# Gated mix of two linear-attention blocks: another PSUM bank for the warm-ups and the gate's turn, and another order of the first k products

## The chip, the cores and the metric

One Trainium2 chip, and of it one core. The metric is the device time of one execution in microseconds (us). The kernel before took 183.33 us, the median of 3 executions (183.22 to 184.1). A profile is one further execution, recorded instruction by instruction; its times are counted from the first instruction of the span.

## The reference

The input `x` has 2048 rows of 640 columns in bf16. Two blocks, A and B, with weights of their own, both read this `x`. Each block makes q, k and v with one product, applies the feature map `phi` to q and k, and does linear attention over 32 heads of 20 columns. A gate, one number for each row, mixes the two results.

```python
g = _sigmoid((x * gate_w).sum(-1, keepdims=True))
a = _A_ref(x, A_wqkv, A_wo)
b = _B_ref(x, B_wqkv, B_wo)
return g * a + (1 - g) * b

# a block (H = 32 heads of Dh = 20):
qkv = (x @ wqkv).reshape(B, S, 3, H, Dh).transpose(2, 0, 3, 1, 4)
q, k, v = qkv[0], qkv[1], qkv[2]
phi = lambda t: jnp.where(t > 0, t + 1, jnp.exp(t)) + 1e-6
pq, pk = phi(q), phi(k)
kv = jnp.einsum("bhsd,bhse->bhde", pk, v)
z = jnp.einsum("bhsd->bhd", pk)
num = jnp.einsum("bhqd,bhde->bhqe", pq, kv)
den = jnp.einsum("bhqd,bhd->bhq", pq, z)[..., None] + 1e-6
return (num / den).transpose(0, 2, 1, 3).reshape(B, S, D) @ wo
```

The gate's logit of a row is the product of that row of `x` with `gate_w`. The kernel gets it as one more column of A's k product.

## The kernel before

`x` is cut into 16 row chunks of 128 (index `i`) and its 640 columns into 5 column chunks of 128 (index `c`). TensorE contracts over the partitions, so every product needs `x` transposed: the tile `xT`, 128 x 5 x 2048. DMA transposes write most of `xT`. The first two row chunks are loaded as they are (`xn`) and turned on TensorE: five 128x128 transposes for each chunk, into the PSUM tiles `turned[0]` and `turned[1]` (named `xt` in the profile), which VectorE copies to `xT` in two pieces each, column chunks 0 and 1 first and 2 to 4 after (`keep`, line 242).

PSUM has eight banks. The pool `psum` gives them out as four slots of two banks (line 55); a tile in a slot may be written only when the tile that had the slot before has been read for the last time. Which instruction has to wait for that is worked out when the program is built. Before the change, slot 3 holds the tile `warm`: seven products of ones with ones (line 160) that keep TensorE at work while the first loads are under way, and later, in the second bank of the same tile, the turned gate column (line 256). Slot 3 is then given to the second chunk's k accumulator (line 260). Slot 2 holds the first chunk's, and slots 0 and 1 hold `turned`.

A k product (`k_mm`, line 214) takes one column chunk of one row chunk as weights and streams 320 columns of `wk[0]`, the weights of A's k; `hf` says which half of its 640 columns, and each half has a PSUM bank of its own. The second half is 321 wide, because column 640 of `wk[0]` holds `gate_w`. A row chunk so takes ten products: five column chunks by two halves.

How that gate column gets there matters below. `gate_w` is loaded as five rows of 128 into a corner of the tile `R` (line 131). `gate_column` (line 162) then turns these 5 rows on TensorE into 128 x 5 in PSUM, copies this to `gsb` with VectorE, and copies it with GpSimd, one column chunk at a time (five copies, line 168), into column 640 of `wk[0]`. Every product of the second half reads that column, so it must not start before GpSimd has written it for its column chunk.

The loads are issued on two queues. SyncE's has: `x` chunk 0, `wk` column chunks 0, 2 and 4, DMA transposes of the chunks 2 and 3, `wq` in three parts, and the other transposes of `x`. ScalarE's has: `x` chunk 1, `wk` column chunk 1, `gate_w`, `wk` column chunk 3.

The stage that the change touches is `k_first` (line 232), written in the order in which it is to run (`tc.manual_schedule`). On TensorE its order before is, with c for column chunk, h for half and i for row chunk: ten transposes; c0 h0 i0; the gate's turn; c1 h0 i0; c0 h0 i1; c1 h0 i1; then c0 and c1 of the second half for both row chunks; c2 in both halves; c3 and c4 of row chunk 0; c3 and c4 of row chunk 1. After these come the row chunks 2 and 3 (`k_chunk`, line 225), and then the q products, first in `q_block` (line 284). On VectorE the order before is: `keep` of c0 and c1 for both row chunks, the copy to `gsb`, `keep` of c2 to c4 for both.

Of the kernel before, what the change touches and what calls it, by code (L numbers as in the profile page):

```python
# [9 lines left out]
FP32 = mybir.dt.float32  # L10
# [6 lines left out]
DT = D // P  # L17
# [3 lines left out]
HB = 512  # L21
# [10 lines left out]
def kernel(  # L32
# [11 lines left out]
    nc = tc.nc  # L44
# [13 lines left out]
    def ps_raw(name, slot=None):  # L58

        if slot is None:  # L60
            slot = turn[0]
            turn[0] = (slot + 1) % 4
        return psum.tile([P, 4 * HB], BF16, tag=f"ps{slot}", name=name)

    def ps(name, slot=None):

        return ps_raw(name, slot).bitcast(FP32).rearrange("p (b n) -> p b n", b=2)
# [85 lines left out]
        )  # L153


    raw = ps_raw("warm", 3)
    warm = raw.bitcast(FP32).rearrange("p (b n) -> p b n", b=2)
    one_l, one_r = [nc.const_aps.tensor(1.0, [P, n], BF16) for n in (P, HB)]
    for n in (HB,) * 6 + (HB // 2,):
        nc.tensor.matmul(warm[:, 0, 0:n], lhsT=one_l, rhs=one_r[:, 0:n], start=True, stop=True)  # L160

    def gate_column(gcol):

        nc.tensor.transpose(out=gcol, in_=grow, identity=ident[0:DT, 0:DT])
        gsb = work.tile([P, DT], BF16, tag="rT", name="gsb")
        nc.vector.tensor_copy(out=gsb[:], in_=gcol)
        for c in range(DT):
            nc.gpsimd.tensor_copy(out=wk[0][:, c, D:D + 1], in_=gsb[:, c:c + 1])
# [45 lines left out]
    def k_mm(b, i, c, pt, hf):  # L214
        w = HF + (hf if b == 0 else 0)
        nc.tensor.matmul(  # L216
            pt[:, hf, 0:w], lhsT=xT[:, c, i * P:(i + 1) * P], rhs=wk[b][:, c, hf * HF:hf * HF + w],
            start=(c == 0), stop=(c == DT - 1),
        )

    def k_done(b, i, pt, lifted=False):
        side = (lambda: nc.scalar.copy(out=logit[:, i:i + 1], in_=pt[:, 1, HF:HF + 1])) if b == 0 else None
        phi(pk[:, i, :].rearrange("p (b n) -> p b n", b=2), pt[:, :, 0:HF], HF, lifted, side)

    def k_chunk(b, i, slot=None, lifted=False):
        pt = ps(f"k{'AB'[b]}", slot)
        for hf in range(2):
            for c in range(DT):
                k_mm(b, i, c, pt, hf)
        k_done(b, i, pt, lifted)  # L230

    def k_first():

        pts = [ps("kA", 2), None]
        turned = [ps_raw("xt", i) for i in range(2)]

        def turn(i):
            for c in range(DT):
                cols = slice(c * P, (c + 1) * P)
                nc.tensor.transpose(out=turned[i][:, cols], in_=xn[:, i, cols], identity=ident[:])  # L240

        def keep(i, lo, hi):
            src = turned[i][:, 0:D].rearrange("p (c n) -> p c n", c=DT)
            nc.vector.tensor_copy(out=xT[:, lo:hi, i * P:(i + 1) * P], in_=src[:, lo:hi])

        def part(cs, hfs, chunks=(0, 1)):
            for c in cs:
                for hf in hfs:
                    for i in chunks:
                        k_mm(0, i, c, pts[i], hf)  # L250

        for i in range(2):
            turn(i)
            keep(i, 0, 2)
        part((0,), (0,), (0,))
        gate_column(raw[:, 2 * HB:2 * HB + DT])
        for i in range(2):
            keep(i, 2, DT)
        part((1,), (0,), (0,))
        pts[1] = ps("kA", 3)  # L260
        part((0, 1), (0,), (1,))
        part((0, 1), (1,))
        part((2,), (0, 1))
        for i in range(2):
            part((3, 4), (0, 1), (i,))
            k_done(0, i, pts[i])
        for i in range(2, CB):
            k_chunk(0, i, i - 2)
# [272 lines left out]
    part = [slice(n * RB, (n + 1) * RB) for n in range(4)]  # L541
# [156 lines left out]
    with tc.manual_schedule():  # L698
        k_first()
# [23 lines left out]
    with tc.manual_schedule():  # L723
# [101 lines left out]
        for i in range(half - 1):  # L825
            p, after = pairs[i:i + 2]
# [48 lines left out]
```

## Time and profile before

| what | us |
|---|---|
| median of 3 executions (183.22, 183.33, 184.1) | 183.33 |
| the profiled execution, from its first to its last instruction (span) | 181.9 |
| what lies around the span, by the median | 1.4 |
| busy time in the span: TensorE products | 177.9 |
| busy time in the span: TensorE weight loads, beside the products | 120.7 |
| busy time in the span: VectorE | 147.2 |
| busy time in the span: ScalarE | 86.3 |
| busy time in the span: GpSimd | 2.5 |

The profiled execution's time is known by its span alone; its share before the first and after the last instruction is taken from the median. PE is TensorE's products, PEld its weight loads, DVE is VectorE, ACT ScalarE, POOL GpSimd, SP SyncE; a q behind an engine's name is its queue or sequencer, which issues DMAs. In a timeline row the first number is when the first instruction of the row started, the second how long the row lasts until its last instruction ends; `xN` is the count. The duration of a product counts from its start to the arrival of its last result, and products overlap, so that the distance between two starts, not the duration, is what one product costs in a stream.

### The profile page before, as it was taken

The page shows a single profiled execution, that of the slowest core. Times are in us where ns is not written, and L with a number is a line of the kernel's source. Part 1 is how long each engine was busy: PE and PEld are TensorE (multiplying, and loading weights), DVE is VectorE, ACT ScalarE, POOL GpSimd, SP SyncE. Part 2 cuts the span into 40 slices and gives each one's busy share as a digit, 9 for nine tenths or more (in the row PEclk, how much of TensorE's full clock was granted, in tenths as well). Part 3 has the DMA queues.
Part 4 walks back from the last instruction along what each step waited for, and adds up shares of the span by engine and source line. Part 5 has one row for each costly group of instructions (what it writes and reads, how often), then busy time and mean ns, then how long its engine had stood idle before and what let it go on. Part 6 is the DMA issues. An engine that isn't in the chain of part 4 may idle for free.

```text
span 181.9 us, 3296 instructions
## 1 busy us (share of the span) xinstructions
PE 177.9 (98%) x1285; PEld 120.7 (66%) x1285; DVE 147.2 (81%) x248; ACT 86.3 (47%) x141; POOL 2.5 (1%) x18
## 2 busy tenths in 40 slices
PE   8999999999999999999999999999999999999993
PEld 3566657765577777877775555577778777777772
DVE  0386868989998896788778999969799999877863
ACT  2245846889961101378784779921102863111010
POOL 4100000000000000000000000000000000000000
PEclk9999999999999999999999999999999999999999
DMA  5899999423100116241115000000343570133323
GB/s 177 207 248 189 224 373 310 85 52 130 58 0 8 67 45 211 77 137 37 56 34 191 17 0 0 0 0 18 126 105 84 174 188 0 40 108 108 114 90 126
DMA packets 22598, 19.17 MB, mean 105 GB/s; under 512 B 10294, under 2 KB 21814, under 8 KB 22582
## 3 DMA queue, kind: packets, MB, share of 16 engines
q1 hardware_dynamic: 20644, 16.82, 33.4%
q10 hardware_dynamic: 1938, 2.13, 3.5%
q8 instruction: 10, 0.16, 0.4%
q14 instruction: 6, 0.05, 0.1%
HBM read 12.13 MB, written 4.53 MB: 92 GB/s over the span
## 4 chain that ended last, share of the span: by engine, by line
PE 95%; DMA 2%; ACTq 0%; DVE 0%; issue 0%
PE gs L369 17%; PE kA L216 12%; PE ox L583 12%; PE kB L216 12%; PE qB L280 12%; PE qA L280 6%; PE oz L583 6%; PE qA L290 5%; PE gB L328 2%; PE gA L328 2%; PE ow L583 2%; DMA R<-in_gate_w_dram 2%; PE qA L300 1%; PE s L485 1%; PE mA L485 1%; PE kvA L455 1%
## 5 line engine op out<-in xcount | busy, mean ns | idle before, releaser
L216 PEld LDWEIGHTS <-xT 128*128 128x128 bf16 x320 | 31.1, 98 | 12.5 <-issue 0.2
L208 DVE TENSOR_SCALAR e<-e 128x640 bf16<-128x640 bf16 (+2 forms) x53 | 18.9, 357 | 8.1 <-ACT e L203 7.4
L216 PE MATMUL kB<-wkB,xT 128*128 128x320 bf16 x160 | 23.0, 299 | 0.0
L216 PE MATMUL kA<-wkA,xT 128*128 128x320 bf16 (+1 forms) x160 | 22.6, 300 | 0.2 <-DMA wkA<-in_A_wqkv_dram 0.2
L280 PE MATMUL qB<-xT,wqB 128*128 128x512 bf16 x100 | 21.7, 379 | 0.0
L203 ACT ACTIVATE e<-kB 128x640 bf16<-128x640 f32 x16 | 11.3, 704 | 16.2 <-DMA wqB<-in_B_wqkv_dram 9.4
L280 PEld LDWEIGHTS <-wqB 128*128 128x128 bf16 x100 | 11.7, 117 | 9.7
L203 ACT ACTIVATE e<-kA 128x640 bf16<-128x640 f32 x16 | 11.2, 705 | 8.5 <-PE kA L216 8.5
L203 ACT ACTIVATE e<-qA 128x1024 bf16<-128x1024 f32 (+1 forms) x11 | 10.4, 946 | 6.4 <-PE qA L290 5.1
L633 ACT COPY u<-ox 128x320 f32<-128x320 f32 x8 | 3.4, 426 | 20.4 <-PE ox L583 20.4
L203 ACT ACTIVATE e<-qB 128x1024 bf16<-128x1024 f32 x10 | 10.2, 1024 | 5.6 <-PE qB L280 4.9
L369 PEld LDWEIGHTS <-xn 128*128 128x128 bf16 x96 | 9.2, 98 | 3.9 <-issue 0.4
L369 PEld LDWEIGHTS <-S 128*128 128x128 bf16 x96 | 9.4, 98 | 3.6
L280 PE MATMUL qA<-xT,wqA 128*128 128x512 bf16 x50 | 11.0, 379 | 0.0
L212 DVE SCALAR_TENSOR_TENSOR pk<-kB,e 128x640 bf16<-128x640 f32 x12 | 9.9, 825 | 1.3
L583 PEld LDWEIGHTS <-xT 128*128 128x128 bf16 x85 | 8.1, 98 | 2.9
L583 PEld LDWEIGHTS <-pqTB 128*128 128x128 bf16 x80 | 7.8, 98 | 3.2
L583 PEld LDWEIGHTS <-pqTA 128*128 128x128 bf16 x80 | 7.7, 98 | 2.9
L369 PE MATMUL gs<-pk,xn 128*128 128x320 bf16 x64 | 9.5, 299 | 0.0
L280 PEld LDWEIGHTS <-wqA 128*128 128x128 bf16 x50 | 5.9, 117 | 4.8
L290 PE MATMUL qA<-xT,wqA 128*128 128x512 bf16 x40 | 9.0, 379 | 0.0
L210 DVE TENSOR_TENSOR pk<-pk,e 128x640 bf16<-128x640 bf16 x12 | 5.9, 493 | 2.8 <-ACT pk L207 2.1
(122 smaller groups left out, 297.7 us busy)
## 6 DMA issues: line engine op xcount, KB each, us to landing
out_dram<-pk SPq DMA_DIRECT2D x14, 160.0 KB, 1.8
xn<-in_A_x_dram SPq DMA_DIRECT2D x3, 640.0 KB, 6.3
wkB<-in_B_wqkv_dram SPq DMA_DIRECT2D x1, 800.0 KB, 4.6
wqB<-in_B_wqkv_dram ACTq DMA_DIRECT2D x1, 800.0 KB, 5.1
wvB<-in_B_wqkv_dram SPq DMA_DIRECT2D x1, 800.0 KB
MA<-mA_dram SPq DMA_DIRECT2D x1, 800.0 KB, 4.2
MB<-mB_dram SPq DMA_DIRECT2D x2, 400.0 KB, 4.5
wqA<-in_A_wqkv_dram SPq DMA_DIRECT2D x2, 320.0 KB, 4.2
```

What stands on the lines that cost most here:

```text
L203: nc.scalar.activation(out=e[:], in_=src, func=ACT.Exp)
L208: nc.vector.tensor_scalar(e[:], e[:], 1.0, EPS, op0=ALU.min, op1=ALU.add)
L210: nc.vector.tensor_tensor(out=dst, in0=dst, in1=e[:], op=ALU.max)
L212: nc.vector.scalar_tensor_tensor(out=dst, in0=src, scalar=1.0 + EPS, in1=e[:], op0=ALU.add, op1=ALU.max)
L216: nc.tensor.matmul(pt[:, hf, 0:w], lhsT=xT[:, c, i * P:(i + 1) * P], rhs=wk[b][:, c, hf * HF:hf * HF + w], start=(c == 0), stop=(c == DT - 1),
L280: nc.tensor.matmul(pt[:, u, :], lhsT=mixed(wq[b][:, c, :], m), rhs=xT[:, c, n * HB:(n + 1) * HB], start=(c == 0), stop=(c == DT - 1),)
L290: nc.tensor.matmul(pt[:, u, :], lhsT=mixed(wq[b][:, c, :], m + u), rhs=xT[:, c, n * HB:(n + 1) * HB], start=(c == 0), stop=(c == DT - 1),)
L328: nc.tensor.matmul(pt[:, hf, 0:HF], lhsT=xn[:, i, c * P:(c + 1) * P], rhs=pk[:, i, hf * HF:(hf + 1) * HF], start=(i == 0), stop=(i == ST - 1),
L369: nc.tensor.matmul(pt[:, n, 0:HF], lhsT=left[:, i, n * P:(n + 1) * P], rhs=right[:, i, :], start=(first and i == 0), stop=(i == hc - 1), s ...
L485: nc.tensor.matmul(dst[:w, 0:HF], lhsT=KVA[:w, k, 0:w], rhs=wo_sb[b][:w, k, n * HF:(n + 1) * HF], start=True, stop=True,)
L583: nc.tensor.matmul(dst, lhsT=left[:, c, r0:r0 + P], rhs=right[:, c, :], start=(first and c == 0), stop=(c == DT - 1), skip_group_check=not ...
L633: nc.scalar.copy(out=self.u6[:], in_=self.at("x"))
```

## The change

The seven warm-up products and the gate's turn now write the second bank of slot 1, the slot of `turned[1]`, whose transposes take only the first bank. Slot 3 has no other tile ahead of the second chunk's k accumulator any more, so both accumulators can be written from the start. The order in `k_first` is new as well. On TensorE: ten transposes; c0 and c1 of the first half for both row chunks (four products); the gate's turn; c2 h0 i0; c0 and c1 of the second half for both row chunks; c2 h0 i1; c2 h1 for both; and then c3 and c4 as before. On VectorE `keep` of c2 to c4 of row chunk 0 now stands ahead of the copy to `gsb`, and that of row chunk 1 behind it. The number of instructions on every engine is the same, and from c3 of row chunk 0 on TensorE's order is as before; ScalarE, GpSimd and SyncE have the same instructions in the same order throughout.

```diff
-    raw = ps_raw("warm", 3)
-    warm = raw.bitcast(FP32).rearrange("p (b n) -> p b n", b=2)
+    opened = [ps("kA", slot) for slot in (3, 2)]
+    pts = opened[::-1]
+    turned = [ps_raw("xt", i) for i in range(2)]
+    warm = turned[1].bitcast(FP32).rearrange("p (b n) -> p b n", b=2)
     one_l, one_r = [nc.const_aps.tensor(1.0, [P, n], BF16) for n in (P, HB)]
     for n in (HB,) * 6 + (HB // 2,):
-        nc.tensor.matmul(warm[:, 0, 0:n], lhsT=one_l, rhs=one_r[:, 0:n], start=True, stop=True)
+        nc.tensor.matmul(warm[:, 1, 0:n], lhsT=one_l, rhs=one_r[:, 0:n], start=True, stop=True)
...
     def k_first():
 
-        pts = [ps("kA", 2), None]
-        turned = [ps_raw("xt", i) for i in range(2)]
-
...
         for i in range(2):
             turn(i)
             keep(i, 0, 2)
-        part((0,), (0,), (0,))
-        gate_column(raw[:, 2 * HB:2 * HB + DT])
-        for i in range(2):
-            keep(i, 2, DT)
-        part((1,), (0,), (0,))
-        pts[1] = ps("kA", 3)
-        part((0, 1), (0,), (1,))
+        part((0, 1), (0,))
+        keep(0, 2, DT)
+        gate_column(turned[1][:, 2 * HB:2 * HB + DT])
+        keep(1, 2, DT)
+        part((2,), (0,), (0,))
         part((0, 1), (1,))
-        part((2,), (0, 1))
+        part((2,), (0,), (1,))
+        part((2,), (1,))
         for i in range(2):
             part((3, 4), (0, 1), (i,))
             k_done(0, i, pts[i])
```

## The prediction

> **What bounds the kernel now.** I read the page first, then the chain of waits, and then the timeline of the one stage that the change touches. On the page TensorE decides:
>
> ```profile
> span 181.9 us, 3296 instructions
> PE 177.9 (98%) x1285; PEld 120.7 (66%) x1285; DVE 147.2 (81%) x248; ACT 86.3 (47%) x141; POOL 2.5 (1%) x18
> ...
> PE 95%; DMA 2%; ACTq 0%; DVE 0%; issue 0%
> ```
>
> TensorE's products are busy for 98% of the span, and the chain that ended last is TensorE for 95% and DMA for 2%. So a time won or lost on TensorE early on goes through to the end, unless a later wait eats it. Nearly all of the DMA's 2% is one load (3.71 of 181.9 us). The start of the chain of waits (start, length, what):
>
> ```profile
> 1.73 3.71 DMA R<-in_gate_w_dram
> 5.44 0.05 issue
> 5.49 0.17 PE warm L164
> 5.66 0.24 PE kA L216
> 5.91 0.01 issue
> 5.92 5.34 PE kA L216 x38
> 11.26 4.32 PE qA L290 x20
> ```
>
> The load of `gate_w`, issued at 1.73, lands at 1.73 + 3.71 = 5.44; the gate's turn starts at 5.49; and from 5.92 TensorE runs without a stop. All that the change can move lies between 5.05 and about 7.3 us. The timeline of that stretch (start, length, engine, line, work, count, idle time before):
>
> ```profile
> 3.62 1.25 PE L240 MATMUL xt<-ident,xn 128*128 128x128 bf16 x10
> ...
> 4.38 0.29 DVE L244 COPY xT<-xt 128x256 bf16<-128x256 bf16 x1 [3.40 <-PE xt L240]
> 4.72 0.10 PEld L216 LDWEIGHTS <-xT 128*128 128x128 bf16 x1
> 4.91 0.29 DVE L244 COPY xT<-xt 128x256 bf16<-128x256 bf16 x1 [0.24 <-PE xt L240]
> 5.05 0.30 PE L216 MATMUL kA<-wkA,xT 128*128 128x320 bf16 x1 [0.17 <-DMA wkA<-in_A_wqkv_dram]
> 5.49 0.09 PEld L164 LDWEIGHTS <-R 5*128 5x128 bf16 x1 [0.66 <-DMA R<-in_gate_w_dram]
> 5.49 0.17 PE L164 MATMUL warm<-ident,R 5*128 5x5 bf16 x1
> ...
> 5.60 1.98 PE L216 MATMUL kA<-wkA,xT 128*128 128x320 bf16 x12
> 5.70 0.16 DVE L166 COPY gsb<-warm 128x5 bf16<-128x5 bf16 x1 [0.50 <-PE warm L164]
> 5.78 0.61 DVE L244 COPY xT<-xt 128x384 bf16<-128x384 bf16 x2
> ...
> 5.93 0.66 POOL L168 COPY wkA<-gsb 128x1 bf16<-128x1 bf16 x5 [3.45 <-DVE gsb L166]
> ```
>
> And single instructions of it, from the same view over a few hundredths of a us each (a product of the first half, GpSimd's first copy, and where the second half and where c3 begin):
>
> ```profile
> 5.60 0.31 PE L216 MATMUL kA<-wkA,xT 128*128 128x320 bf16 x1
> 5.93 0.19 POOL L168 COPY wkA<-gsb 128x1 bf16<-128x1 bf16 x1 [3.45 <-DVE gsb L166]
> 6.19 0.43 PE L216 MATMUL kA<-wkA,xT 128*128 128x321 bf16 x2
> 7.28 0.44 PE L216 MATMUL kA<-wkA,xT 128*128 128x320 bf16 x2
> ```
>
> Read in order: product 1 at 5.05, the gate at 5.49, product 2 at 5.60, product 3 at 5.92, product 5, the first of the second half, at 6.19, product 13, the first of c3, at 7.28. From product 5 to 13 are eight steps in 7.28 - 6.19 = 1.09 us: **0.136 us is what a k product costs** in a stream (its 0.30 us of duration overlap). Twelve products at that price are 1.63 us; the stretch from 5.05 to 7.28 takes 2.23. So TensorE stands still for about 0.6 us, less the gate's own slot (5.60 - 5.49 = 0.11): **0.49 us is what the stretch could give** at most.
>
> Where that stands: from 5.05 + 0.14 = 5.19 to 5.49, 0.30 us, TensorE has only the gate next, whose weights come by DMA; from 5.60 + 0.14 = 5.74 to 5.92, 0.18 us, product 3 waits until slot 3 is free, that is for the copy to `gsb`, which ends at 5.70 + 0.16 = 5.86.
>
> **The change part by part.** *The spare bank.* The seven warm-ups and the gate's turn are the same instructions at another address, and before the transposes nothing else touches slot 1: 0. Product 3's wait for slot 3 goes.
>
> *Four products ahead of the gate.* Product 1 stays at 5.05, because it waits for `wk` column chunk 0. The second is now c0 of row chunk 1, and its weights come with VectorE's second copy, which ends at 4.91 + 0.29 = 5.20. From the first such copy's end, 4.38 + 0.29 = 4.67, to the weight load at 4.72 it took 0.05, so product 2 starts at 5.25. The third needs `wk` column chunk 1. Its issue, and the answer for that issue in the view of DMAs (last number: us to landing):
>
> ```profile
> 1.24 0.46 ACTq L123 DMA_DIRECT2D wkA<-in_A_wqkv_dram x1
> wkA<-in_A_wqkv_dram ACTq DMA_DIRECT2D x1, 160.0 KB, 4.0
> ```
>
> It lands at 1.24 + 4.0 = 5.24, before it is wanted: products 3 and 4 start at 5.39 and 5.53, and the gate's turn at **5.66** in place of 5.49. `gate_w` has long landed then (5.44).
>
> *VectorE.* The copy that now stands ahead of `gsb` is one of 384 columns. Two of them took 0.61 us, so one at most 0.35. It can start when the 256-column copy ends at 5.20 and is done by 5.55, before the gate is turned; so it does not hold up `gsb`. The other moves behind `gsb`, ends near 6.3, and is wanted for the eleventh product only, at about 6.9.
>
> *The product that fills in.* After the gate comes c2 h0 i0, at 5.66 + 0.11 = 5.77. Its weights are there at 5.55 + 0.05 = 5.60. Its `wk` column chunk 2:
>
> ```profile
> 1.73 0.42 SPq L123 DMA_DIRECT2D wkA<-in_A_wqkv_dram x1
> wkA<-in_A_wqkv_dram SPq DMA_DIRECT2D x1, 160.0 KB, 3.9
> ```
>
> 1.73 + 3.9 = 5.63, in time. TensorE is free again at 5.77 + 0.14 = 5.91.
>
> *What is late next: the gate column.* The sixth product is the first of the second half, and it reads the column that GpSimd writes. Before, from the gate's start to the end of GpSimd's first copy it took 5.93 + 0.19 - 5.49 = 0.63 us, by way of `gsb` at 5.70. With a semaphore's 0.05 the column could be read at 6.17, and the product that reads it began at 6.19: a wait without cost, with 0.02 to spare. Now the same 0.68 us count from 5.66, and the column can be read at **6.34**, while TensorE is free at 5.91. So a new wait of **0.43 us** stands where the two old gaps (0.30 and 0.18) were. Behind it in TensorE's queue are all the others; none can pass. GpSimd's further copies follow at (0.66 - 0.19) / 4 = 0.12 us, faster than TensorE asks for them, and cost nothing.
>
> *The sum.* Seven products stand between that wait and c3: c0 and c1 of the second half (four), c2 h0 i1, c2 h1 for both. 6.34 + 7 x 0.136 = 7.29. Before it was 7.28. **The stage ends within 0.02 us of where it ended**: the gate begins 0.17 later, and against this one product fewer (0.136) is left to do behind the gate column. From c3 on the order is as before. Against the profiled execution that is 181.9 + 0.02 = 181.9 in the span, and with the 1.4 us around it, 183.33 - 181.9, **183.35** against the median of the three runs.
>
> *Bounds.* From below: were TensorE never to wait after 5.25, c3 would begin at 5.77 + 8 x 0.136 = 6.86, 0.42 earlier. That can't be reached while the second half reads a column that comes 0.68 us behind the gate. From above: the gate's turn now stands behind `wk` column chunk 1, which in the shown run came 0.15 before it was wanted. Were it to land as late as the next one, 5.63, products 3 and 4 would start at 5.68 and 5.82, the gate at 5.95, and c3 at 5.95 + 0.68 + 0.95 = 7.58, 0.30 later. So the stage itself lies between -0.42 and +0.30.
>
> **What could hide a gain, or make a loss larger.** The q products follow at 11.09 to 11.26. The first part of their weights:
>
> ```profile
> 6.50 0.58 SPq L136 DMA_DIRECT2D wqA<-in_A_wqkv_dram x1
> wqA<-in_A_wqkv_dram SPq DMA_DIRECT2D x1, 320.0 KB, 4.2
> ```
>
> They land at 6.50 + 4.2 = 10.7, so up to about 0.4 us of gain would meet no wait there; a forecast of 0 never comes near it. SyncE's queue waits only for landings and not for TensorE, so no transfer moves.
>
> **The clock.** TensorE's rate changes within this stretch, though the page grants 1.00 throughout. The seven warm-ups, the q products at full stream, the last warm-up alone, and one stage of the view of windows (stage and its length, busy PE, PEld, DVE, ACT, POOL, then the granted clock):
>
> ```profile
> 0.84 2.93 PE L160 MATMUL warm<-const-bfloat16-1.0 128*128 128x512 bf16 x7 [0.84 <-PEq L859]
> 11.09 4.48 PE L290 MATMUL qA<-xT,wqA 128*128 128x512 bf16 x20
> ...
> 3.35 0.42 PE L160 MATMUL warm<-const-bfloat16-1.0 128*128 128x256 bf16 x1
> ...
> 3.00:4.00 1.00, 1.00 (x7) 0.46 (x6) 0.00 (x0) 1.00 (x1) 0.00 (x0) 1.00 1.04 342
> ```
>
> A warm-up costs about (2.93 - 0.42) / 6 = 0.42 us for 512 columns, a q product 4.32 / 20 = 0.216. So TensorE started at half its rate, and the k products at 0.30 us each ran at the full one already at 5.05. Up to there both kernels issue the same work at the same times. The Trainium skill, "TensorE: Matmul & The Clock Gate", Part 1, tells of a clock that is doubled only after a busy window of some 3.4 us that runs freely, whatever the kernel does, and halved after an idle one; the trace agrees as to the step of two and its time. By that rule a pause of half a microsecond changes nothing, but a window that is judged too idle would put off the full rate by another one, 1.7 us at half price, or 185.0 as an estimate.
>
> **The rivals.**
>
> *A. Even trade* (forecast): as summed, 183.35, c3 within 0.1 us of 7.28. For it: the times of the five links from the gate to the column stand in the trace, and they are latencies of idle engines, not shares of busy ones.
>
> *B. A net gain of 0.1 to 0.4 us, 183.0 to 183.2.* If `gate_w` lands later in most executions than in this one, say after 5.62, the gate starts at the same time in both kernels, and the change keeps one product fewer behind it: 0.14 us. More would need a shorter way from the gate to the column, for which no row speaks.
>
> *C. It doesn't do what it says: fewer than four products are ahead in time*, because column chunk 1 of `wk` or the second copy is late and the gate waits behind them: +0.1 to +0.3, 183.45 to 183.65. For it: the margin is 0.15 us on a transfer that takes 4.0. Against it: it is issued 0.49 us before `gate_w`.
>
> *D. Slower beyond doubt: the full rate comes later.* The change puts one pause of 0.43 us in place of 0.30 and 0.18. If what decides on the clock looked at that very stretch, the products after 5.91 would run at half rate, and each us of that costs 0.5. A loss of 0.92 us needs 1.84 us of it. As long a stretch again as from the first warm-up to the first product at full rate, 5.05 - 0.84 = 4.2 us, would cost 2.1: 185.4. Against it: the full rate was there at 5.05, and afterwards pauses of 0.30 and 0.18 us didn't end it.
>
> *E. Faster beyond doubt*: the same the other way round. One of the three runs before took 184.1, 0.8 more than the others; if that were a later full rate and the change made it rarer, the median would still be 183.2 to 183.3. So 0.9 us is not to be had here, other than by a cause that I don't see.
>
> **How the numbers follow.** Chances: A 0.62, B 0.12, C 0.16, D 0.06, E 0.04. About 0.5% of the time, 0.92 us, is what a measurement of this kernel can tell from no change: the three runs before differ by 0.88. A, B and C all lie within it, 0.90 together; D is slower, E faster. The range: A to C give 183.0 to 183.65; the runs before spread from 183.22 to 184.1 without any change, so I take 182.8 to 184.0.
>
> **What would show it.** In the profile of the changed kernel: the gate's turn near 5.66 and no longer in a pause; a pause of some 0.4 us on TensorE ahead of the first 321-wide product, put down to GpSimd's copy or to issue; that product near 6.34; c3 of row chunk 0 near 7.29; q products from 11.1 on as before. Wrong would be: c3 before 7.1 or after 7.5, k products 0.27 us apart in place of 0.136 after 5.05, or a new wait after 7.3.

## The result, and the profile after

| | before | changed |
|---|---|---|
| median, us (22 executions each) | 183.38 (183.05 to 184.1) | 183.91 (183.32 to 184.38) |
| ratio to before, 95% interval | | 1.0025 (1.0015 to 1.0034) |
| profiled execution: span, us | 181.9 | 182.4 |
| profiled execution: time, us | not listed | 184.13 |

The forecast was 183.35, no change, with a range of 182.8 to 184.0. The time lies in the range and within 0.5%, but the change is slower by 0.28 to 0.62 us, which repeated executions do tell from zero. The range held the time only because it had been widened by the scatter of the runs before: the rivals A to C alone ended at 183.65.

The page of the changed kernel (it has five product records fewer than the page of before, at the same number of weight loads):

```profile
span 182.4 us, 3291 instructions
...
PE 178.1 (98%) x1280; PEld 120.7 (66%) x1285; DVE 147.2 (81%) x248; ACT 86.2 (47%) x141; POOL 2.5 (1%) x18
...
PE 94%; issue 3%; POOL 1%; DVE 0%; POOLq 0%
```

TensorE still decides. In place of the DMA's 2%, the chain's start is now put down to issue and to GpSimd, as the end of that start in the chain of waits shows (start, length, what):

```profile
2.47 4.16 issue
6.63 0.21 POOLq L868
6.84 0.04 issue
6.88 4.93 PE kA L218 x35
```

TensorE's unbroken stream begins at 6.88, not at 5.92, and what it waited for is GpSimd's copy of the gate column. (The link from there to `gsb` is lost in this view; the timeline has it.) The timeline of the stage in the changed kernel:

```profile
4.75 1.51 PE L218 MATMUL kA<-wkA,xT 128*128 128x320 bf16 x4
4.94 0.56 DVE L243 COPY xT<-xt 128x256 bf16<-128x256 bf16 x2 [0.24 <-PE xt L239]
5.28 0.40 PEld L218 LDWEIGHTS <-xT 128*128 128x128 bf16 x3 [0.43 <-DVE xT L243]
6.19 0.10 PEld L166 LDWEIGHTS <-R 5*128 5x128 bf16 x1 [0.52 <-issue]
6.20 0.18 PE L166 MATMUL xt<-ident,R 5*128 5x5 bf16 x1
...
6.31 0.31 PE L218 MATMUL kA<-wkA,xT 128*128 128x320 bf16 x1
6.42 0.17 DVE L168 COPY gsb<-xt 128x5 bf16<-128x5 bf16 x1 [0.93 <-PE xt L166]
...
6.65 0.66 POOL L170 COPY wkA<-gsb 128x1 bf16<-128x1 bf16 x5 [4.18 <-DVE gsb L168]
6.88 1.39 PE L218 MATMUL kA<-wkA,xT 128*128 128x321 bf16 x9 [0.26 <-POOL wkA L170]
```

The order is the forecast's: four products, the gate, one product, a wait for GpSimd, the second half. The times are not. The four products take 1.51 us from start to end where four at full rate without a wait take about 0.7 (3 x 0.136 + 0.30): the second waits for VectorE's second copy until 5.28, and the others run at half rate. The gate's turn starts at 6.20, where 5.66 was forecast. It waits for no load: its weights stand behind "issue". In this execution `gate_w` had landed at 4.68, by the trace's semaphore events, which the views list only where something waits for them. Before, it had landed at 5.44.

All of the difference lies in this stage. The first product of row chunk 2, one instruction each from the timelines of the kernel before and of the changed one:

```profile
8.37 0.57 PE L216 MATMUL kA<-wkA,xT 128*128 128x320 bf16 x3
```

```profile
8.93 0.57 PE L218 MATMUL kA<-wkA,xT 128*128 128x320 bf16 x3
```

8.93 - 8.37 = 0.56, and the spans differ by 0.55. Behind that product, span less start, it is 173.49 us in both; in all the 14 profiles of this study it lies between 173.48 and 173.57. Each profile can therefore be read by its first nine microseconds alone:

| profile | `gate_w` landed | full rate from | gate's turn | first 321-wide | c3 | row chunk 2 |
|---|---|---|---|---|---|---|
| before | 5.44 | 4.82 | 5.49 | 6.19 | 7.28 | 8.37 |
| e5, before again | 4.83 | 4.43 | 5.14 | 5.84 | 6.93 | 8.02 |
| changed | 4.68 | 6.35 | 6.20 | 6.88 | 7.84 | 8.93 |
| e4, changed again | 4.67 | 4.16 | 5.51 | 6.19 | 7.14 | 8.23 |
| e1, gate first | 4.80 | 5.81 | 5.42 | 6.33 | 7.29 | 8.38 |
| e2, gate after one | 4.76 | 6.24 | 5.37 | 6.38 | 7.33 | 8.43 |
| e3, gate after two | 4.80 | 5.75 | 5.70 | 6.55 | 7.50 | 8.60 |
| e6, after one, slot 0 | 4.54 | 3.83 | 4.77 | 5.86 | 6.81 | 7.93 |
| e7, no column read | 4.71 | 4.05 | 5.43 | 5.79 | 6.73 | 8.04 |
| e8, 128-row gate | 4.67 | 6.57 | 6.16 | 6.88 | 7.83 | 8.93 |
| e9, before, late `gate_w` | 6.45 | 4.16, again 10.99 | 6.50 | 7.20 | 8.96 | 11.05 |
| e10, changed, late `gate_w` | 6.95 | 5.57 | 7.00 | 7.67 | 8.63 | 9.72 |
| e11, before, one warm-up | 4.64 | about 7.1 | 5.16 | 6.08 | 7.70 | 8.79 |
| e12, changed, one warm-up | 4.80 | about 7.5 | 6.26 | 6.95 | 8.14 | 9.23 |

The full rate's start is the trace's clock event. For e11 and e12 it is read from the distance of the products. In e7's row the product under "first 321-wide" is 320 wide.

### The profile page after: what moved, and what is told of

Its sections match the earlier page's. It is cut to its first block, busy times and chain, and to the rows that moved or that the text cites. A ratio compares the mean times of both kernels' runs of the same rounds, so it can differ in the third digit from the quotient of the medians.

```text
span 182.4 us, 3291 instructions
## 1 busy us (share of the span) xinstructions
PE 178.1 (98%) x1280; PEld 120.7 (66%) x1285; DVE 147.2 (81%) x248; ACT 86.2 (47%) x141; POOL 2.5 (1%) x18
## 4 chain that ended last, share of the span: by engine, by line
PE 94%; issue 3%; POOL 1%; DVE 0%; POOLq 0%
PE gs L367 17%; PE ox L581 12%; PE kB L218 12%; PE qB L278 12%; PE kA L218 12%; PE qA L278 6%; PE oz L581 6%; PE qA L288 5%; PE gB L326 2%; PE gA L326 2%; PE ow L581 2%; PE qA L298 1%; PE s L483 1%; PE mA L483 1%; PE kvA L453 1%
## 5 line engine op out<-in xcount | busy, mean ns | idle before, releaser
L218 PE MATMUL kA<-wkA,xT 128*128 128x320 bf16 (+1 forms) x160 | 23.3, 304 | 0.3 <-POOL wkA L170 0.3
```

The costliest lines, as they stand in the source:

```text
L218: nc.tensor.matmul(pt[:, hf, 0:w], lhsT=xT[:, c, i * P:(i + 1) * P], rhs=wk[b][:, c, hf * HF:hf * HF + w], start=(c == 0), stop=(c == DT - 1),
```

## The experiments

Two theories stood against each other at first. "Place": what stands ahead of the gate's turn on TensorE delays the gate column, and the second half waits for that. "Clock": the new bank or the new pause puts off TensorE's full rate.

**e1, e2, e3: the gate's turn behind none, one and two products, spare bank and own slots kept; e4: the changed kernel again.** The three edits in one, abridged:

```diff
+        gate_column(...)            # e1: here
         part((0,), (0,), (0,))
+        gate_column(...)            # e2: here
         part((0,), (0,), (1,))
+        gate_column(...)            # e3: here
         part((1,), (0,))
         keep(0, 2, DT)
-        gate_column(turned[1][:, 2 * HB:2 * HB + DT])
```

In e1 to e3 both `keep` of c2 to c4 follow the gate.

> Spare bank and own slots as in the change, but the gate's turn ahead of all k products. Theory 'place' (the gate column is what the second half waits for, and what stands ahead of the gate's turn on TensorE decides): the gate starts as soon as gate_w has landed (4.7 to 5.4 us), first 321-wide product near 6.3, c3 near 7.25, time -0.15 to 0.0 us against the kernel before, about 0.5 us under the changed kernel. Theory 'clock' (warm-ups and gate's turn in the other bank put off TensorE's full rate): +0.3 to +0.6 us against before, as the changed kernel, with k products still 0.27 us apart after 5.3.

> Spare bank and own slots as in the change, the gate's turn behind one k product as before the change, then the other three, c2 h0 i0 and the second half. 'Place': gate at 5.1 to 5.5, no wait for GpSimd's column, c3 near 7.1 to 7.3, -0.16 to -0.05 us against before. 'Clock': +0.3 to +0.6 us.

> The same with two k products ahead of the gate's turn. 'Place': between e2 and the changed kernel, -0.15 to +0.1 us against before; where TensorE is at half rate by then the gate starts near 5.7. 'Clock': +0.3 to +0.6 us.

> The changed kernel once more, on the same chip as the three others, to have its times beside theirs and a second profile of it. Both theories: +0.3 to +0.6 us against before. 'Place': whether the profile shows the four products 0.27 or 0.136 us apart depends on when the full rate comes in that execution; the gate starts near 6.2 where they are 0.27 apart, near 5.7 to 5.8 where they are not. 'Clock': the full rate comes after 6 us again.

| | median, us | ratio to before, 95% interval |
|---|---|---|
| e1, gate first | 183.53 | 1.0027 (1.0001 to 1.0052) |
| e2, after one | 183.39 | 1.0004 (0.9992 to 1.0015) |
| e3, after two | 183.77 | 1.0017 (1.0008 to 1.0027) |
| e4, after four, the change | 183.62 | 1.0017 (1.0006 to 1.0029) |

(Before, on the same chip: 183.34.) With one product ahead the time is that of before; with two and four it is slower. With none the interval only just leaves 1 out. The spare bank and the own slots, which e2 has as well, don't by themselves make the change's loss: "clock" as the banks' doing falls. The full rate came at 5.81, 6.24, 5.75 and 4.16 us in the four profiles, the earliest in the changed kernel itself, so the change does not force the 6.35 of its first profile.

Three of the four sizes were missed all the same: e2 didn't gain its 0.05 to 0.16 us, e1 gained nothing, and e3 lost as much as the change. Not all of e3's loss is its two products:

```profile
6.15 0.66 POOL L170 COPY wkA<-gsb 128x1 bf16<-128x1 bf16 x5 [3.68 <-DVE gsb L168]
6.40 1.07 PEld L218 LDWEIGHTS <-xT 128*128 128x128 bf16 x9 [0.47 <-DVE xT L243]
```

The fill-in product c2 h0 i0 had to wait for VectorE's copy, which in e3 stands behind the one to `gsb`, and started at 6.40. The column could be read near 6.39 (6.15 + 0.19, and 0.05 from the copy's end to its reader), so by an estimate from these rows about 0.16 us of e3's loss, the first 321-wide product at 6.55 and not at 6.39, belongs to VectorE's order.

e1's timeline shows why the gate is not early there:

```profile
4.96 0.10 PEld L166 LDWEIGHTS <-R 5*128 5x128 bf16 x1 [0.20 <-DMA R<-in_gate_w_dram]
5.07 0.29 DVE L243 COPY xT<-xt 128x256 bf16<-128x256 bf16 x1 [0.24 <-PE xt L239]
5.42 0.16 PE L166 MATMUL xt<-ident,R 5*128 5x5 bf16 x1 [0.38 <-DVE xT L243]
```

The weights are in at 4.96, but the turn waits 0.38 us for VectorE's second copy, which still reads the other bank of the same tile. That is a cost of the spare bank that the prediction had put at 0. The change's own order doesn't pay it, because its second product waits for the same copy anyway. Why two of e1's twelve executions took 185.45 and 185.48 stays open; one of the eleven of e5, the kernel before unaltered, took 185.57.

e4's time is as expected; its gate, expected at 5.7 to 5.8 where the full rate comes early, started at 5.51. Its timeline has the changed kernel at full rate from its first product on:

```profile
4.72 0.86 PE L218 MATMUL kA<-wkA,xT 128*128 128x320 bf16 x4
...
5.51 0.09 PEld L166 LDWEIGHTS <-R 5*128 5x128 bf16 x1 [0.26 <-issue]
5.51 0.17 PE L166 MATMUL xt<-ident,R 5*128 5x5 bf16 x1
...
5.72 0.16 DVE L168 COPY gsb<-xt 128x5 bf16<-128x5 bf16 x1 [0.52 <-PE xt L166]
...
5.94 1.64 PE L218 MATMUL kA<-wkA,xT 128*128 128x320 bf16 x10 [0.25 <-DVE gsb L168]
...
5.95 0.66 POOL L170 COPY wkA<-gsb 128x1 bf16<-128x1 bf16 x5 [3.48 <-DVE gsb L168]
```

Here the four products take 0.86, and the gate starts at 5.51 though `gate_w` had been there since 4.67. (The 0.25 ahead of the fifth product ended with `wk` column chunk 2, landed at 5.90; the view names `gsb`, done at 5.88.)

**e5: the kernel before, unaltered, to see whether its first profile was typical.**

> The kernel before once more, as it stands: what two sets of times of one kernel differ by, and a second profile. Theory 'landing' (in the profile that the prediction was made from, gate_w landed at 5.44 us, later than in most executions; in the five profiles since it landed at 4.67 to 4.80): gate_w near 4.7, the gate's turn at 5.0 to 5.2 instead of 5.49, the first 321-wide product near 5.9 to 6.2 and c3 of row chunk 0 at 7.0 to 7.4, the later the later the full rate comes. Rival 'order alone' (landing as in the first profile, the changed kernel loses elsewhere): gate at 5.49 again. Time: within 0.15 us of the kernel before.

Median 183.44 (before, in this set: 183.34), ratio 1.0014 (0.9993 to 1.0036): two sets of one kernel. Its timeline:

```profile
4.90 0.31 PE L216 MATMUL kA<-wkA,xT 128*128 128x320 bf16 x1
5.14 0.09 PEld L164 LDWEIGHTS <-R 5*128 5x128 bf16 x1
5.14 0.17 PE L164 MATMUL warm<-ident,R 5*128 5x5 bf16 x1
...
5.25 2.39 PE L216 MATMUL kA<-wkA,xT 128*128 128x320 bf16 x15
5.35 0.16 DVE L166 COPY gsb<-warm 128x5 bf16<-128x5 bf16 x1 [0.21 <-PE warm L164]
...
5.58 0.66 POOL L168 COPY wkA<-gsb 128x1 bf16<-128x1 bf16 x5 [3.10 <-DVE gsb L166]
```

The gate starts at 5.14 and waits for no load; the first 321-wide product and c3 come 0.06 and 0.07 us before the times named. `gate_w` landed at 4.83 here. Twelve profiles issue that load where the kernel before does; in eleven of them it landed at 4.54 to 4.83, and the twelfth is the one that the prediction was read from. This execution took 183.34 us, the median of before; its span is 181.6.

**e6: as e2, the gate's turn in the second bank of slot 0.**

```diff
-        gate_column(turned[1][:, 2 * HB:2 * HB + DT])
+        gate_column(turned[0][:, 2 * HB:2 * HB + DT])
```

> As e2, gate's turn behind one k product, but written into the second bank of slot 0 (the first chunk's transposes) in place of slot 1. In e1 and e2 the gate's turn waited for VectorE's second copy out of slot 1, to 5.37 and 5.42 us, though gate_w had landed at 4.8. 'Landing': the gate starts at 5.0 to 5.2, 0.2 earlier than in e2, and the stage has no wait left behind it: c3 at 7.0 to 7.25, -0.2 to 0.0 us against before, the fastest so far. Rival 'gate doesn't matter': as e2, +0.07 us.

Median 183.25, ratio 0.9998 (0.9983 to 1.0012). The gate starts at 4.77, with no wait for VectorE, and c3 at 6.81, the earliest of all kernels that read the column:

```profile
4.77 0.17 PE L166 MATMUL xt<-ident,R 5*128 5x5 bf16 x1
```

Both came earlier than named. So the wait in e1 and e2 was the shared tile's. The time is the lowest median of the experiments, but no difference to before can be told. Its interval lies below the changed kernel's (1.0015 to 1.0034) and overlaps e4's (1.0006 to 1.0029), so that it beats the changed kernel is likely, and that it beats before is not shown.

**e7: the second half of the first two row chunks 320 wide.** It leaves out the gate's logits of 256 rows, with the two ScalarE copies that fetch them.

```diff
-        w = HF + (hf if b == 0 else 0)
+        w = HF + (hf if b == 0 and i > 1 else 0)
...
-        side = (lambda: ...) if b == 0 else None
+        side = (lambda: ...) if b == 0 and i > 1 else None
```

> The changed kernel, but the second half of the first two row chunks is 320 wide and so doesn't read the gate column (the gate's logits of these 256 rows are left out, with the two copies that fetch them). 'Landing' and 'place': the wait of 0.3 to 0.6 us ahead of the second half goes, c3 0.25 to 0.6 us earlier than in the changed kernel, time -0.3 to +0.1 us against before. Rival 'half rate' (the loss is that more products run at half rate): no such gain, +0.3 us or more.

Median 183.44, ratio 0.9995 (0.9973 to 1.0017). With the gate as late as in e4 (5.43), c3 comes 0.41 us earlier (6.73 against 7.14): the column's wait is where the stage loses. Not all of the 0.41 is the column's, since loads and first products scatter (`wk` column chunk 2 landed at 5.61 here and at 5.90 in e4). Within e7 the column could have been read 0.68 behind the gate, at 6.11, and the product started at 5.79: 0.32 us. The time alone doesn't show it: the interval touches the changed kernel's. Half of the gain is given back at once:

```profile
8.04 0.39 PEld L218 LDWEIGHTS <-xT 128*128 128x128 bf16 x4 [0.39 <-DMA xT<-in_A_x_dram]
```

Row chunk 2 waits for its DMA transpose, landed at 7.99 here and at 7.44 to 8.0 in all profiles. That is the next wall. By an estimate from these landings (0.05 from landing to start, and 8 x 0.136 from c3 to row chunk 2), a c3 earlier than 6.4 (landing at 7.44) to 6.95 (landing at 8.0) brings nothing.

**e8: the gate's turn with 128 rows of weights.**

```diff
+    nc.vector.memset(R[0][:, 0:P], 0.0)
-        nc.tensor.transpose(out=gcol, in_=grow, identity=ident[0:DT, 0:DT])
+        nc.tensor.matmul(gcol, lhsT=R[0][:, 0:P], rhs=ident[:, 0:DT], start=True, stop=True)
...
-        gate_column(turned[1][:, 2 * HB:2 * HB + DT])
+        gate_column(warm[:, 1, 0:DT])
```

> The changed kernel, but the gate's turn is a plain product with all 128 rows (the corner of R is zeroed first, five columns of the identity are streamed). In both profiles of the changed kernel the gate's turn, whose weights have 5 rows, started 0.09 to 0.14 us later behind the product ahead of it than the next k product would. Theory 'drain' (its 5-row weights wait until that product has left the array): the gate starts 0.1 us earlier and the time falls by 0.1 us against the changed kernel. Rival: the distance stays, and so does the time. Either way most of the loss stays: +0.1 to +0.45 us against before.

Median 183.93, ratio 1.0028 (1.0015 to 1.0041). The gate's turn in its timeline:

```profile
5.90 0.15 PEld L167 LDWEIGHTS <-R 128*128 128x128 bf16 x1
6.16 0.21 PE L167 MATMUL xt<-ident,R 128*128 128x5 bf16 x1
```

The distance from the fourth product's start to the gate's was 0.41 us in the changed kernel's profile and is 0.27 here, both at half rate; its weights load at 5.90, during the product before. So "drain" is right about the distance, though e8 changes two things at once, the number of rows and a transposition into a plain product. The time didn't fall: from the gate to the column it took 0.72 in place of 0.69, and the remaining 0.1 us is less than the interval.

**e9 and e10: before and changed, `gate_w` issued behind `wk` column chunk 3.**

```diff
-        if c == 1:
+        if c == 3:
             nc.scalar.dma_start(out=grow, in_=gate_w.rearrange("(c p) -> c p", p=P))
```

> The kernel before, with gate_w issued behind wk's column chunk 3 on ScalarE's queue, so that it lands near 5.3 us and not near 4.7. Theory 'landing': this brings back the case that the prediction was worked out for. The gate's turn starts at 5.35 to 5.5 (5.14 in e5), c3 at 7.1 to 7.5, and the time rises by 0.1 to 0.35 us against the kernel before. Rival (the gate's landing doesn't decide): c3 at 6.9 to 7.0 where the full rate comes early, and no change of the time.

> The changed kernel with the same late gate_w. 'Landing': its gate is later than the load anyway, behind four products, so nothing changes for it: gate at 5.5 to 5.7 with an early full rate, at 6.2 with a late one, c3 at 7.15 to 7.85, the time as that of the changed kernel (+0.3 to +0.5 us against before), and the distance to e9 only 0.0 to 0.3 us. Rival: as far from e9 as the changed kernel is from before, 0.3 to 0.5 us.

The load came far later than meant, at 6.45 and 6.95 us and not at 5.3. Before: 185.89 (6 executions), ratio 1.0118 (1.0088 to 1.0147) to the kernel before of this set, 183.47. Changed: 184.79 (11 executions), ratio 1.0074 (1.0039 to 1.0109). **By the medians the sign turns**: with `gate_w` that late the changed kernel is the faster one, by about 1 us. The intervals overlap. The granted clock divides both sets: two of e9's executions and four of e10's had a mean clock of 0.991, and these don't differ (186.24 and 186.25 against 185.94 to 186.54). Among the others, at 0.998 to 1.000, all seven of e10 (183.77 to 184.91) lie below all four of e9 (185.07 to 185.95). Both expectations named too small an effect, and the price of e9 is not the wait alone. Its timeline, and its windows (stage and length, busy PE, PEld, DVE, ACT, POOL, then the granted clock):

```profile
4.79 0.30 PE L216 MATMUL kA<-wkA,xT 128*128 128x320 bf16 x1 [0.20 <-DMA wkA<-in_A_wqkv_dram]
6.50 0.17 PE L164 MATMUL warm<-ident,R 5*128 5x5 bf16 x1 [1.41 <-DMA R<-in_gate_w_dram]
6.60 4.61 PE L216 MATMUL kA<-wkA,xT 128*128 128x320 bf16 x19
```

```profile
4.20:7.60 3.40, 1.78 (x15) 0.99 (x13) 1.26 (x5) 0.00 (x0) 0.66 (x5) 1.00 1.08 227
7.60:11.00 3.40, 3.40 (x15) 1.96 (x13) 0.00 (x0) 0.73 (x2) 0.00 (x0) 0.50 0.94 266
11.00:14.40 3.40, 3.40 (x25) 2.33 (x23) 2.98 (x6) 1.96 (x6) 0.00 (x0) 1.00 1.10 202
```

After a pause of 1.41 us the granted clock falls to 0.50 for 3.4 us. In e10 the four products fill part of the pause, 1.01 us of it are left, and the clock of its profile stays at 1.00:

```profile
7.00 0.17 PE L166 MATMUL xt<-ident,R 5*128 5x5 bf16 x1 [1.01 <-DMA R<-in_gate_w_dram]
```

The four executions at 0.991 speak for a fall there too, though no profile of one is on record.

**e11 and e12: before and changed, one warm-up of 256 columns.**

```diff
-    for n in (HB,) * 6 + (HB // 2,):
+    for n in (HB // 2,):
```

> The kernel before with one short warm-up product in place of seven, so that TensorE runs at half rate through all of this stage. 'Place' with its half rate: gate at 5.1 to 5.2, the first 321-wide product near 6.1, eight steps of 0.267 from there: c3 near 8.25. The time is 1 to 3 us above before, and scatters.

> The changed kernel with one short warm-up product. 'Place' with its half rate: four products 0.27 us apart, gate at 6.1 to 6.2, first 321-wide product near 6.9, seven steps of 0.267: c3 near 8.75, 0.5 us later than in e11, and the time likewise 0.3 to 0.7 us above e11's. Rival 'what is left at half rate evens it out' (one product fewer behind the gate is worth 0.27 there): 0.0 to 0.2 us.

Before: 184.73, ratio 1.0060 (1.0037 to 1.0083). Changed: 185.1, ratio 1.0095 (1.0066 to 1.0123). Both are against 183.47. The same rows of the two timelines, e11 first:

```profile
5.16 0.18 PE L164 MATMUL warm<-ident,R 5*128 5x5 bf16 x1
...
5.61 0.66 POOL L168 COPY wkA<-gsb 128x1 bf16<-128x1 bf16 x5 [3.14 <-DVE gsb L166]
```

```profile
4.82 1.51 PE L218 MATMUL kA<-wkA,xT 128*128 128x320 bf16 x4
...
6.26 0.18 PE L166 MATMUL xt<-ident,R 5*128 5x5 bf16 x1
...
6.71 0.66 POOL L170 COPY wkA<-gsb 128x1 bf16<-128x1 bf16 x5 [4.24 <-DVE gsb L168]
```

At half rate the gate is put off by 1.10 us and the column with it. c3 is 0.44 us later (8.14 against 7.70), where 0.5 was expected; the medians differ by 0.37, with intervals that overlap. Both profiles reached the full rate before c3, sooner than expected, so c3 itself came earlier than named.

## Why the prediction was right in its kind and short in its size

- *What bounds the kernel: right.* Only this stage moved; behind row chunk 2's first product every profile has 173.5 us.
- *Its own signs of being wrong* showed in the first profile: c3 at 7.84, after 7.5, and products 0.24 to 0.27 apart after 5.05. In e4 they didn't: c3 at 7.14 and products 0.14 apart. That the time stayed in the range all the same owes something to luck, because the width came from the scatter of three runs and not from this term.
- *The median: a small error.* I took 183.33 - 181.9 = 1.4 us to lie around the span. The later executions list both: 184.13 - 182.4 = 1.7. So the profiled execution had taken about 183.6, more than the median, and its late `gate_w` is one reason: e5, at the median, has c3 0.35 us earlier.
- *Four products ahead of the gate: the term that was mis-sized.* "The gate's turn at 5.66 in place of 5.49", +0.17, was worked out from a load that lands at 5.44 and products at 0.136. Of two executions at full rate there, e5 and e4, it is 5.14 to 5.51: **+0.37**. Of e11 and e12, both at half rate there, 5.16 to 6.26: **+1.10**. The start of the first product scatters (4.90 in e5, 4.72 in e4); counted from it, the forecast had the gate at 0.61 in place of 0.44, and the runs have 0.79 (e4) in place of 0.24 (e5) at full rate and 1.45 (the changed profile) in place of 0.38 (e11) at half. Three things make the sizes. `gate_w` usually lands some 0.7 us earlier, so that before the change the gate had been held up by TensorE's own order and hardly by the load: 0.24 in place of 0.44. Product 2 waits for VectorE's second copy, 0.28 behind product 1 in e4 and 0.53 in the changed profile where 0.20 was forecast, and products 2 to 4 are 0.24 to 0.27 us apart where the full rate hasn't come. And the gate's 5-row weights wait for the product ahead to leave, 0.09 to 0.14 us, which the profile of before could not show, where the turn followed a pause. This last one stands in both orders (0.24 behind product 1 in e5, 0.23 behind product 4 in e4), so it makes the forecast of 5.66 too early, but no difference between the kernels.
- *The wait that takes the old gaps' place: right.* GpSimd's column, 0.43 forecast; in the changed profile 6.88 - 6.31 - 0.136 = 0.43, of which the view, which counts from the end of the product ahead, puts 0.26 down to GpSimd. In e4 it is 0.11, because the fill-in product waited for `wk` column chunk 2 until 5.94; e7 takes the wait away, which is worth 0.32 there. From the gate to the first 321-wide product 0.68 was forecast, and e4 has 0.68, the changed profile 0.69.
- *One product fewer behind the column: right.* Seven steps to c3: 7.84 - 6.88 = 0.96, against eight before. So the loss is what the gate is late, less one product: 0.37 - 0.136 = 0.23, and 7.14 - 6.93 = 0.21 was measured between e4 and e5. Where the full rate comes late, part of the larger delay is made up, because more of what is left then runs at the full rate: seven steps took 8.14 - 6.95 = 1.19 us in e12 and eight 7.70 - 6.08 = 1.62 in e11, and c3 is 0.44 late. Counted from each profile's first product, c3 is 0.39 late at full rate (2.42 in e4, 2.03 in e5) and 0.40 at half (3.32 in e12, 2.92 in e11). The measured 0.28 to 0.62 us holds both; with one pair of profiles for each rate, that this is the whole of it is argued and not shown.
- *Rival C* (slower by 0.1 to 0.3, gate behind a late column chunk) had the sign and nearly the size, and half of its cause: `wk` column chunk 1 was not late (4.90 in the changed profile), but at half rate the second copy was, and product 2 started 0.53 behind product 1 where 0.20 was forecast.
- *Rival B* (late `gate_w`, so a gain) needs a load that the kernel doesn't usually have: in e9 and e10, where it lands after 6 us, the medians turn the sign, by far more than the 0.14 that I gave it, with the clock's part in it.
- *Rival D* (the full rate comes later): not by this change, as far as the profiles show. The start of the full rate scatters from 3.83 to 6.57 us over the twelve profiles with seven warm-ups. The three with the order of before have 4.16 to 4.82, the nine with the spare bank 3.83 to 6.57, too few to tell a difference. But the clock's events lie on one grid: in eleven of the twelve, the last fall comes 177.49 or 177.50 us after the first rise, and in e9 180.91, which are 52 and 53 steps of 3.413. All twelve first rises lie within one such step, so none of them shows a rise put off by a step. The rival's mechanism exists, though: e9 shows a pause that costs the rate. The pause of 0.43 us did not: in the changed profile the rate rose at 6.35, just ahead of it, and stayed.

## What to carry to other kernels

Work put ahead of the head of a chain that runs over several engines (here TensorE, VectorE, GpSimd and back) delays its end, by what that work takes and by what it waits for; fill work belongs behind the head. Before a load's landing becomes a term in a sum, look at it in a second execution: here one profile had it some 0.7 us late, and with that the change looked nearly free. And in the first microseconds, price TensorE's work at both of its rates.

## What the runs showed of the hardware

The start of TensorE's full rate scatters by 2.7 us between executions of nearly the same work (3.83 to 6.57 us), within one step of a grid of 3.413 us. In e9 it came at 4.16, went at 7.58 and came back at 10.99, two steps of 3.41 us. The Trainium skill, "TensorE: Matmul & The Clock Gate", Part 1, has a window of about 3.4 us that runs freely; the trace agrees. But it asks for an idle window before the rate is halved, and in e9 1.78 us of products (transpositions among them) in the 3.40 before the fall, with one pause of 1.41, didn't hold it. A 5-row weight load isn't taken ahead as 128-row ones are: it started 0.41 us behind the previous product's start where a 128-row one allowed 0.27 (changed kernel and e8, at half rate; e8's is also a plain product and no transposition).
